# A 3136-point spectral block: the forward 49-point stage folded over n2 and -n2, in 50x50 products on quarters of the TensorE array

## The chip, the cores and the metric

One Trainium2 chip, one core. The metric is the device time of one execution in microseconds (us); the kernel before has a median of 1829.1 us over 3 runs (1829.03 to 1830.06). Everything is held and multiplied in 32-bit floats. The engines go by their names in the profile: PE is TensorE (matmul), PEld its weight loads, DVE VectorE, ACT ScalarE, POOL GpSimd, SP SyncE, which issues nearly all DMAs here.

## The reference, cut to what matters

The input x is 8 x 3136 x 256. A spectral filter runs along the sequence (a real FFT of 3136 points, a complex 256 x 256 product per frequency, a soft threshold, the inverse FFT); a second part takes the real part of a 2-D FFT of its result, normalises and applies a two-layer MLP.

```python
X = np.fft.rfft(x, axis=1)
Yr = X.real @ w_r - X.imag @ w_i + b_r
Yi = X.real @ w_i + X.imag @ w_r + b_i
Yr, Yi = shrink(Yr, 0.01), shrink(Yi, 0.01)
y = np.fft.irfft(Yr + 1j * Yi, n=3136, axis=1)
u = y + np.real(np.fft.fft(np.fft.fft(y, axis=1), axis=2))
un = (u - mean(u)) / sqrt(var(u) + 1e-6)
out = u + np.maximum(un @ w_ch1, 0) @ w_ch2
```

## The kernel before, in words

The 3136 points are taken as n = 49 n1 + n2, with 64 values of n1 and 49 of n2. For each of the 8 batches (`b`) these steps run; all of them are generators whose steps are put in order by due times (`T` is one batch in those units), and a scheduling layer that knows the waits then fixes one static order on each engine.

- **f1** (`p1`, and `p1_first` for the first batch): the 64-point transform over n1. `x` is loaded with n1 on the partitions (two halves of 64, for two sets of n2) into `xf`, multiplied by the table `fwd_f`, copied out of PSUM to `ev` (L522) and stored to DRAM as `ad`. From batch 2 on most f1 steps run as *quarter products* (`quads`, `run_quads`): four 64x64 products that use four quarters of the array at once, together with the four of an inverse step g1, under one start (L377 is the first product, L382 the others). Ahead of such a set `pair` writes one column of each of its two PSUM banks (L370) on DVE, so that the first product waits for both banks.
- **f2** (`p2_f2`): the 49-point transform over n2, for 32 values `u`. In each of 4 steps `q` it loads eight values of u: `af` (L584; 98 partitions, which are n2 by real and imaginary part, by 4 u x 256 channels) and the table `tff` (L580; 98 x 4 x 100). Each of `ui` = 0..3 fills one bank `g_f2` with four matmuls at L606: stationary `af` (98 x 128 channels), moving `tff` (98 x 100, real and imaginary outputs of 50 slots). A 32-bit matmul stands in the trace as two instructions, so 512 matmuls are 1024 rows of L606. Each bank is copied (`xx`, L629, or `im`, L644), split into a high part (`Xh`, L620) and a low part (`Xl`, L162 on POOL or L159 on DVE), and summed (`xs`, L636 or L645).
- **w** (`p2_w`): the 256 x 256 complex product, three terms each through `mm3` (L165 to L167).
- **mix, yt, g2, g1** (`p2_mix`, `p2_yt`, `p2_g2`, `p3_norm`): the channel FFT and the inverse transforms, with DRAM round trips `md`, `bd`. `bev` (L887) is the copy that is stored to `bd` (L889).
- **MLP** (`p3_tr`, `p3_mlp1`, `p3_mlp2`): `h` = W1 products (6 of 128x512 for one of eight `f`), ACT makes `hh` (L1055), DVE makes `hl` (L1056), and the 12 products into `o` use both.

The profile strips numbers from names: `g_f` is a bank of f1 or f2, `g_g` one of g1 or g2, `a` the `ad` of the first batch. All these banks come from one ring of four (`gtile`). The waits of one engine are in order: an instruction that waits holds all that stand behind it on that engine. SP is one such queue for loads and stores alike.

The lines that the steps of the prediction speak of, as they stand before:

```python
g = gtile("g_f2")
for s in range(2):
    for k in range(2):
        te.matmul(o, afs[s][:, ui * D + k * 128:ui * D + k * 128 + 128],
                  tfs[s][:, ui].rearrange("p (c j) -> p c j", c=2), start=True, stop=True)
```

Of the kernel before, what the change touches and what calls it, by code (L numbers as in the profile page):

```python
# [55 lines left out]
def rows_n2():  # L56

    return np.append(np.arange(48).reshape(2, 24).T.reshape(-1), 48)


def tables():
# [3 lines left out]
    fwd = np.zeros((2, N1, 2, 2, U))  # L65
    inv = np.zeros((2, 2, U, 2, 2, 32))
    n1h = rows_n1()
    for s in range(2):
        for u in range(U):
            ph = 2 * np.pi * ((n1 * u) % N1) / N1  # L70
            if u == 0:
                alt = np.where(n1 % 2, -1.0, 1.0)
                fwd[s, :, s, 0, 0] = 1.0
                fwd[s, :, s, 1, 0] = alt
                inv[s, 0, 0, :, s] = 1.0
                inv[s, 1, 0, :, s] = np.where(n1h % 2, -1.0, 1.0)
            else:
                fwd[s, :, s, 0, u] = np.cos(ph)
                fwd[s, :, s, 1, u] = -np.sin(ph)
# [3 lines left out]
    tf = np.zeros((2, N2, U, 2, S))  # L83
    ti = np.zeros((2, S, U, 2, N2))
    for u in range(U):
        t, sg = slot_freqs(u)
        m = len(t)
        ph = 2 * np.pi * (np.outer(n2, t) % N) / N
        co, si = np.cos(ph), np.sin(ph)
        if u == 0:  # L90
            for c in range(2):
                j = slice(25 * c, 25 * c + 25)
                tf[c, :, 0, 0, j] = co[:, j]
                tf[c, :, 0, 1, j] = -si[:, j]
                w = np.full(25, 2.0)
                w[0 if c == 0 else 24] = 1.0
                ti[0, j, 0, c] = (co[:, j] * w).T / N
                ti[1, j, 0, c] = (-si[:, j] * w).T / N
        else:
            tf[0, :, u, 0, :m] = co  # L100
            tf[1, :, u, 0, :m] = si
            tf[0, :, u, 1, :m] = -si * sg
            tf[1, :, u, 1, :m] = co * sg
            ti[0, :m, u, 0] = co.T / N
            ti[1, :m, u, 0] = -(si * sg).T / N
            ti[0, :m, u, 1] = si.T / N
            ti[1, :m, u, 1] = (co * sg).T / N
# [10 lines left out]
        tf=tf[:, rows_n2()].transpose(1, 0, 2, 3, 4).reshape(98, U, 100),  # L118
# [18 lines left out]
TURN = 0.2  # L137
EARLY, HALF = (2.03, 2.2, 2.36), 0.03
# [4 lines left out]
def spectral_block(ctx: ExitStack, tc: tile.TileContext, x, w_ri, b_ri, w1, w2,  # L143
# [123 lines left out]
    def load_tf():  # L267
        yield 0.31 * T
        for s in range(2):
            tff = sb.tile([98, 4, 100], F32, tag="tff", bufs=3, name="tff")  # L270
# [72 lines left out]
    def a_rows(t, n0, n):  # L343

        return t[n0 % 24:n0 % 24 + n, n0 // 24].rearrange("m c u d -> (c u) m d") if n0 < 48 else t[24:25, 0].rearrange("m c u d -> (c u) m d")

    def x_rows(b, m, n):

        if m == N2 - 1:
            return [xv[b + r][:, m:m + 1] for r in range(2)]  # L350
        return [xv[b][:, 24 * r + m:24 * r + m + n] for r in range(2)]

    def quads(gs, table, src):

        ops = []
        for k in range(2):
            rows = slice(64 * k, 64 * k + 64)
            for p in range(2):
                m = src[rows, p]
                o = gs[k][64 * p:64 * p + 64, :m.shape[1] * D].rearrange("q (i d) -> q i d", d=D)  # L360
                ops.insert(0, (o, table[rows, rows], m))
# [10 lines left out]
    def run_quads(ops, marks, key=None):  # L372
# [4 lines left out]
        mm = te.matmul(*ops[0], start=True, stop=True)  # L377
# [6 lines left out]
    chunks = [(m, 2) for m in range(0, NM - 1, 2)]  # L384

    def p1_first():
# [21 lines left out]
        todo = chunks + [(N2 - 1, 1)]  # L408
        xfs = []
        for (m, n), (tag, bufs, z, i) in zip(todo, slots):  # L410
            if i == 0:
                xf = sb.tile([128, z * 512], F32, tag=tag, bufs=bufs, name="xf")
            for r, src in enumerate(x_rows(0, m, n)):
                ld = (nc.scalar if r else nc.sync).dma_start(out=xf[r * 64:r * 64 + 64, i * 512:i * 512 + n * D], in_=src).ins
# [3 lines left out]
        for ci, (m, n) in enumerate(todo):  # L418
# [7 lines left out]
            mm = te.matmul(g[:, :w], fwd_0, xf[:, i * 512:i * 512 + w], start=True, stop=True)  # L426
# [6 lines left out]
            if i == z - 1:  # L433
# [3 lines left out]
                if n == 1:  # L437
                    for k, t in enumerate((a0, a8, a16, a24)):
                        o, i_ = t[24, 0].rearrange("c u d -> (c u) d"), ev[32 * k:32 * k + 16, :D]
# [4 lines left out]
                    for k in range(4):  # L444
                        later[3].append((ad1[24, 0, :, 8 * k:8 * k + 8], ev[32 * k + 16:32 * k + 32, :D]))
                    continue
                for k, t in enumerate((a0, a8, a16, a24)):
                    o, i_ = t[mb:mb + nn].rearrange("m r c u d -> (r c u) m d"), v[32 * k:32 * k + 32]
# [12 lines left out]
    def p1(b):  # L461
# [19 lines left out]

        def load(k):

            xfs[k] = sb.tile([128, 1024], F32, tag="x4", bufs=2, name="xf")
            for r in range(2):
                rows = slice(64 * r, 64 * r + 64)
                if k == 6:
                    behind(7, out=xfs[k][rows, :D], in_=xv[b + r][:, N2 - 1:])
                else:
                    ld = behind(5 if b == 1 else "mt" if b == 2 else 7, out=xfs[k][rows], in_=xv[b][:, 8 * k + 4 * r:8 * k + 4 * r + 4])  # L490
# [7 lines left out]
        for i, (t, k) in enumerate(order):  # L498
            yield t
            while b == 1 and (0, 2, 2) not in f2_mm:  # L500
# [4 lines left out]
            w = D if k == 6 else 512  # L505
            whole = k == 6 or b == 1 or keys[k] is None
            if not whole:
                gs, marks = pair("g_f1")
                waiting[keys[k]] = quads(gs, fwd_f, xf.rearrange("q (p i d) -> q p i d", p=2, d=D)), marks
# [3 lines left out]
            for r in range(2 - (k == 6)):  # L513
                if whole:
                    yield t + (F1_STEP if b == 1 else HALF) * T * r
                    g = gtile("g_f1")
                    with tc.issue_after(f2_mm[0, 2, 2]) if b == 1 and k == r == 0 else nullcontext():
                        te.matmul(g[:, :w], fwd_f, xf[:, r * 512:r * 512 + w], start=True, stop=True)
# [3 lines left out]
                (va.tensor_copy if r and whole and b > 1 else sc.copy)(ev[:, :w], g[:, :w])  # L522
                for p in range(2):
                    n2, n = 8 * k + (4 * p + 2 * r if whole else 4 * r + 2 * p), 2
                    ad = a_dram[b](0)[0]
                    if k == 6:
                        ad, n2, n = a_dram[b + p](0)[0], N2 - 1, 1
                    st_eng.dma_start(out=a_rows(ad, n2, n),
                                     in_=ev[p * 64:p * 64 + 64, :w].rearrange("p (n d) -> p n d", d=D))
# [25 lines left out]
    def p2_f2(b):  # L555


        for q in range(4):
# [6 lines left out]
            for s in range(2):  # L565
                roomy = b == 0 and q == 2
                if roomy:
                    if s == 0:
                        wide = sb.tile([98, 8 * D], F32, tag="mq", bufs=2, name="af")
                    af = wide[:, s * 4 * D:(s + 1) * 4 * D]  # L570
                else:
                    af = sb.tile([98, 4 * D], F32, tag="af", bufs=3, name="af")
# [3 lines left out]
                if not (b == q == 0):  # L576
                    tag, bufs = ("eo", 2) if roomy else ("bev", 3) if b == 0 and q == s == 1 else ("tff", 3)
                    tff = sb.tile([98, 4, 100], F32, tag=tag, bufs=bufs, name="tff")
# [4 lines left out]
                with tc.issue_after(af_ld["mt" if b else ("st", q - 1)]) if held else nullcontext():  # L583
                    ld = nc.sync.dma_start(out=af, in_=ad[:, :, :, u:u + 4].rearrange("m r c u d -> (m r c) (u d)")[0:98])  # L584
# [9 lines left out]
            for ui in range(4):  # L594
                yield base + STEP * ui * F2W / 4
                if b == 0 and q == 1:
                    yield from after(("w", 0))
                us = slice(ui * 2, ui * 2 + 2)
                g = gtile("g_f2")
                gv = g[:, :400].rearrange("p (k c t) -> p k c t", k=2, c=2)  # L600
                for s in range(2):
                    yield base + STEP * F2W * (ui / 4 + s / 8)
                    for k in range(2):
                        o = gv[:, k, :, s * S:s * S + S]
                        with tc.issue_after(last_mix[0]) if b == 1 and q == ui == 0 else behind_w(0, b == 0 and q == 1 and ui == 0):
                            f2_mm[b, q, ui] = te.matmul(o, afs[s][:, ui * D + k * 128:ui * D + k * 128 + 128], tfs[s][:, ui].rearrange("p (c j) -> p c j", c=2),  # L606
                                      start=True, stop=True).ins
                def put(f, outs, *ins, us=us):

                    both = len(outs[0]) == 1  # L610
                    for k in range(1 if both else 2):
                        v = [(t[0] if both else t[k])[..., us, :] for t in outs]
                        if not both:
                            i_ = [i[:, k] for i in ins]
                            d = "p u j -> p (u j)" if len(v[0].shape) == 3 else "p c u j -> p c (u j)"
                        else:
                            i_ = ins
                            d = "p k u j -> p k (u j)" if len(v[0].shape) == 4 else "p k c u j -> p k c (u j)"
                        v = [t.rearrange(d) for t in v]
                        res = f(v[0], *i_, *v[1:])  # L620
                    return res

                xs = sb.tile([128, 2, 2 * S], F32, tag="xs", bufs=2, name="xs")
                first = b == 1 and q == 0
                lag = b < 2 and q == 0
                if ui < (3 if b and not first else 2):
                    xx = sb.tile([128, 2, 2, 2 * S], F32, tag="xx", bufs=2, name="xx")
                    with tc.issue_after(ends["mix"][0]) if first else nullcontext():
# [540 lines left out]
```

## Time and profile before

| | us |
|---|---|
| median of 3 runs | 1829.1 |
| the profiled execution | 1830.16 |
| its span, first to last instruction | 1828.4 |
| PE busy | 1810.3 |
| DVE busy | 1179.5 |
| ACT busy | 834.6 |
| POOL busy | 370.3 |

The profiled execution is 1.1 us above the median, and 1.8 us of it lie outside the span. Shares of busy time are averages over the span; which engine sets the end in a stage is read from a table by stage (busy time of each engine in a window) and from the chain of waits, which goes back from the last instruction to what released each one. Ends of matmuls are modelled, so starts are the surer reading.

### The profile page before, as it was taken

What the parts mean: (1) busy time and instruction counts of PE and PEld (TensorE: products, weight loads), DVE (VectorE), ACT (ScalarE), POOL (GpSimd) and SP (SyncE); (2) the same over time, 40 slices, a digit from 0 to 9 for tenths busy, and PEclk for the clock granted to TensorE, in tenths of its full rate; (3) what the DMA queues carried; (4) which work ended last, traced back from release to release, by engine and by line L of the source; (5) the groups of instructions that cost most, each with busy time, mean ns of one, the idle gap of its engine ahead of it and who ended that gap; (6) DMA issues with size and microseconds to landing.
All of it is one profiled execution on the core that took longest, in us unless ns stands there. A gap on an engine that the chain in (4) does not pass through costs nothing.

```text
span 1828.4 us, 33511 instructions
## 1 busy us (share of the span) xinstructions
PE 1810.3 (99%) x12192; PEld 1597.3 (87%) x12192; DVE 1179.5 (65%) x2754; ACT 834.6 (46%) x1839; POOL 370.3 (20%) x805
## 2 busy tenths in 40 slices
PE   9999999999999999999999999999999999999999
PEld 6777889988999888988888988899899989888888
DVE  4776676766666766667666765766666667655442
ACT  3775554544444544444444444544444444422221
POOL 1522222221122222112222111222121222010000
PEclk9999999999999999999999999999999999999999
DMA  8879563544436453455434535454332543152100
GB/s 237 249 212 216 162 176 118 146 126 117 137 100 165 128 139 107 123 146 152 129 94 130 158 103 141 132 145 123 105 102 82 143 110 91 48 138 61 52 16 35
DMA packets 154877, 232.92 MB, mean 127 GB/s; under 512 B 18192, under 2 KB 108888, under 8 KB 154712
## 3 DMA queue, kind: packets, MB, share of 16 engines
q1 hardware_dynamic: 153672, 229.14, 44.8%
q8 instruction: 96, 1.57, 0.4%
q10 hardware_dynamic: 1040, 1.64, 0.3%
q14 instruction: 69, 0.57, 0.1%
HBM read 127.95 MB, written 102.76 MB: 126 GB/s over the span
## 4 chain that ended last, share of the span: by engine, by line
PE 95%; DVE 2%; DMA 1%; SPq 1%; ACT 1%; issue 0%; DVEq 0%; ACTq 0%
PE o L165 10%; PE o L166 10%; PE h L165 10%; PE h L167 10%; PE h L166 10%; PE o L167 10%; PE g_f L606 5%; PE g_w L165 4%; PE g_w L167 3%; PE g_w L166 3%; PE g_yt L854 3%; PE g_g L377 3%; PE g_ut L1030 2%; PE g_mix L771 2%; PE g_f L382 2%; PE g_g L165 1%
## 5 line engine op out<-in xcount | busy, mean ns | idle before, releaser
L1056 DVE SCALAR_TENSOR_TENSOR hl<-h,hh 128x512 fp32r<-128x512 f32 x392 | 269.9, 689 | 412.3 <-ACT hh L1055 410.3
L1055 ACT ACTIVATE hh<-h 128x512 fp32r<-128x512 f32 x392 | 234.3, 598 | 469.4 <-PE h L167 449.0
L166 PE MATMUL o<-w2h,hl 128*128 128x256 f32 x1568 | 432.0, 285 | 0.9 <-DVE hl L1056 0.9
L167 PE MATMUL o<-w2h,hh 128*128 128x256 f32 x1568 | 423.0, 280 | 0.0
L165 PE MATMUL o<-w2l,hh 128*128 128x256 f32 x1568 | 397.2, 287 | 0.0
L165 PEld LDWEIGHTS o<-w2l,hh 128*128 128x128 f32 x1568 | 283.6, 189 | 43.1 <-issue 23.5
L165 PE MATMUL h<-utl,w1h 128*128 128x512 f32 x784 | 314.4, 401 | 0.3 <-DVE utl L159 0.3
L167 PE MATMUL h<-uth,w1h 128*128 128x512 f32 x784 | 311.0, 397 | 0.0
L166 PE MATMUL h<-uth,w1l 128*128 128x512 f32 x784 | 310.5, 396 | 0.0
L166 PEld LDWEIGHTS o<-w2h,hl 128*128 128x128 f32 x1568 | 295.4, 188 | 6.9 <-DVE hl L1056 1.1
L167 PEld LDWEIGHTS o<-w2h,hh 128*128 128x128 f32 x1568 | 295.4, 188 | 2.7 <-issue 0.5
L167 PEld LDWEIGHTS h<-uth,w1h 128*128 128x128 f32 x784 | 147.4, 188 | 29.7 <-issue 1.1
L165 PEld LDWEIGHTS h<-utl,w1h 128*128 128x128 f32 x784 | 147.5, 188 | 21.4 <-DVE hl L1056 4.1
L166 PEld LDWEIGHTS h<-uth,w1l 128*128 128x128 f32 x784 | 147.7, 188 | 16.4 <-issue 0.2
L959 POOL TENSOR_SCALAR vv<-ag 128x2 f32<-128x2 f32 x98 | 18.9, 193 | 644.4 <-DVE ag L956 639.0
L606 PEld LDWEIGHTS g_f<-tff,af 98*128 98x128 f32 x1024 | 135.5, 192 | 9.3 <-issue 1.4
L606 PE MATMUL g_f<-tff,af 98*128 98x100 f32 x1024 | 140.5, 271 | 1.8 <-DMA af<-a 1.0
L162 POOL TENSOR_TENSOR Xl<-xx,Xh 128x400 fp32r<-128x400 f32 (+1 forms) x95 | 98.1, 1034 | 180.7 <-ACT Xh L620 177.8
L711 ACT ACTIVATE r<-g_w,two_t 128x400 f32<-128x400 f32 x128 | 76.1, 594 | 75.3 <-DVE g_w L707 71.0
L162 POOL TENSOR_TENSOR Xsl<-xs,Xsh 128x200 fp32r<-128x200 f32 x112 | 74.1, 664 | 166.7 <-ACT Xsh L620 163.0
L707 DVE SCALAR_TENSOR_TENSOR g_w<-g_w,bias,ks 128x400 f32<-128x400 f32 x128 | 81.4, 636 | 36.1 <-PE g_w L167 31.5
L159 DVE TENSOR_TENSOR yl<-g_yt,yh 100x512 fp32r<-100x512 f32 x112 | 76.6, 684 | 21.1 <-ACT yh L865 20.2
(160 smaller groups left out, 3281.0 us busy)
## 6 DMA issues: line engine op xcount, KB each, us to landing
bd<-bev SPq DMA_DIRECT2D x128, 196.0 KB
out_dram<-ut SPq DMA_DIRECT2D x98, 256.0 KB
bf<-bd SPq DMA_DIRECT2D x96, 256.0 KB
mt<-md SPq DMA_DIRECT2D x192, 128.0 KB
af<-ad SPq DMA_DIRECT2D x56, 392.0 KB
xf<-in_x SPq DMA_DIRECT2D x84, 256.0 KB
ad<-ev SPq DMA_DIRECT2D x168, 128.0 KB
md<-mq SPq DMA_DIRECT2D x112, 192.0 KB
```

The source lines that it names most:

```text
L159: return va.tensor_sub(out_, full, hi.bitcast(F32))
L162: gp.tensor_sub(out_, full, hi.bitcast(F32))
L165: te.matmul(o, lh, rl, start=start, stop=False)
L166: te.matmul(o, ll, rh, start=False, stop=False)
L167: return te.matmul(o, lh, rh, start=False, stop=stop)
L377: mm = te.matmul(*ops[0], start=True, stop=True)
L606: f2_mm[b, q, ui] = te.matmul(o, afs[s][:, ui * D + k * 128:ui * D + k * 128 + 128], tfs[s][:, ui].rearrange("p (c j) -> p c j", c=2), sta ...
L707: va.scalar_tensor_tensor(gw, gw, bias[:, c, o:o + 1], ks, op0=ALU.add, op1=ALU.add)
L711: ra = sc.activation(r, gw, AF.Relu, bias=lam_t)
L854: te.transpose(gt[:100, (v * 2 + o) * 128:(v * 2 + o + 1) * 128], y[:, o, place].rearrange("p c j -> p (c j)"), ident)
L1055: sc.activation(hh[:, :w], h[:, :w], AF.Relu)
L1056: dv = va.scalar_tensor_tensor(hl[:, :w], h[:, :w], 0.0, hh[:, :w].bitcast(F32), op0=ALU.max, op1=ALU.subtract)
```

## The change

The real input makes the terms n2 and -n2 = 49 - n2 combine: with e = x[n2] + x[-n2] and o = x[n2] - x[-n2], the 49 terms become 25 of e and 24 of o, each used with a cosine or a sine alone.

- **f2**: `af` and `tff` now hold 50 rows at partition 0 and 50 at partition 64 (the two come from the two kinds of output of f1), and a step `q` has two blocks `bi` in place of four `ui`. A block takes two banks at once (`pair`, with its two memsets), real outputs in one, imaginary in the other, and issues 32 quarter products (50 rows, 64 channels, 50 slots) through `run_quads`, one behind the other. Evictions work on 400 columns: copies `xi` and (first block) `xr`, then `Xh`, `Xl`, `xs`, `Xsh`, `Xsl`.
- **f1**: `xf` now pairs rows n2 and -n2 (the second read backwards). Where f1 runs as one 128-row product the table does the fold; where it runs as quarter products DVE does it (L517, L518: two instructions of 128x512, `FOLD` ahead of the step), and the load of `xf` is eight DMAs in place of two, since -n1 has an edge row. The single n2 = 0 (k = 6) is a product of 64 rows by 512 columns in place of 128 by 256.
- **DMAs**: `af` is two DMAs of 50 partitions in place of one of 98; the stores of `ev` are two per f1 step in place of four; `tff` has half the columns.

```diff
@@ tables()
-            tf[0, :, u, 0, :m] = co
-            tf[1, :, u, 0, :m] = si
-            tf[0, :, u, 1, :m] = -si * sg
-            tf[1, :, u, 1, :m] = co * sg
+            tf[0, 0:50:2, u, :z] = cm
+            tf[0, 1:50:2, u, :z] = sm
+            tf[1, 0:50:2, u, :z] = cm * sg
+            tf[1, 1:50:2, u, :z] = -sm * sg
...
+FOLD = 0.05
@@ run_quads
-    def run_quads(ops, marks, key=None):
+    def run_quads(ops, marks=(), key=None, last=None):
...
-        with tc.issue_after(mm.ins), tc.high_priority():
-            for o in ops[1:]:
-                te.matmul(*o, start=True, stop=True)
+        for o in ops[1:]:
+            with tc.issue_after(mm.ins), tc.high_priority():
+                mm = te.matmul(*o, start=True, stop=True)
+        return mm.ins
@@ p1: load
+            else:
+                for r in range(2):
+                    one, two = pairs(b, 4 * k + 1 + 2 * r, 2)[::1 - 2 * r]
+                    behind(key, out=xf[64 * r:64 * r + 64, 0:512], in_=one)
+                    lo, at = 64 * r, 512
+                    to, edge = (lo + 1, (lo, 63)) if r == 0 else (lo, (lo + 63, 0))
+                    behind(key, out=xf[to:to + 63, at:], in_=two[r:r + 63])
+                    for i in range(2):
+                        behind(key, out=xf[edge[0]:edge[0] + 1, at + i * D:at + i * D + D], in_=two[edge[1]:edge[1] + 1, i:i + 1])
@@ p1
+            if not whole(k):
+                yield t - FOLD * T
+                e, o = xfs[k][:, 0:512], xfs[k][:, 512:]
+                va.tensor_add(e, e, o)
+                va.scalar_tensor_tensor(o, o, -2.0, e, op0=ALU.mult, op1=ALU.add)
@@ p2_f2
-                    ld = nc.sync.dma_start(out=af, in_=ad[:, :, :, u:u + 4].rearrange("m r c u d -> (m r c) (u d)")[0:98])
+                    for h in range(2):
+                        ld = nc.sync.dma_start(out=af[64 * h:64 * h + 50], in_=ad[:, :, h, u:u + 4].rearrange("m t u d -> (m t) (u d)"))
...
-            for ui in range(4):
...
-                g = gtile("g_f2")
...
+            for bi in range(2):
...
+                gs, marks = pair("g_f2")
+                ops = []
+                for ui, s, k in ((ui, s, k) for ui in (2 * bi, 2 * bi + 1) for s in range(2) for k in range(2)):
+                    at, d0 = k * 4 * S + (2 * (ui % 2) + s) * S, ui * D + k * 128
+                    for h, p in ((h, p) for p in range(2) for h in range(2)):
+                        rows = slice(64 * h, 64 * h + 50)
+                        ops.append((gs[h][64 * p:64 * p + 64, at:at + S], afs[s][rows, d0 + 64 * p:d0 + 64 * p + 64], tfs[s][rows, ui]))
...
+                f2_mm[b, q, bi] = run_quads(ops, marks, last=behind_mm)
```

How this moves the static order is seen at two places, both in batch 4, step q = 2.

On PE before, the third of the four banks of this f2 step (`g_f_10629`), with what stands around it; `h`, `hh`, `hl`, `o` are the MLP's tiles:

```order
L167 MATMUL h<-uth,w1h 128x512
L606 MATMUL g_f_10629<-tff,af 128x2x50 [waits DVE_49]
L606 MATMUL g_f_10629<-tff,af 128x2x50 x3
L1030 MATMUL g_ut<-ident,ut 128x128 [waits DVE_49]
L165 MATMUL o<-w2l,hh 128x256 [waits Activation_49]
L165 MATMUL o<-w2l,hh 128x256
L1030 MATMUL g_ut<-ident,ut 128x128 x3
L166 MATMUL o<-w2h,hl 128x256 [waits DVE_49]
```

On PE now, the second block of the same step; the banks are `g_f_11549` and `g_f_11550`, and between the two parts shown stand 26 more rows like the four ahead of the cut:

```order
L165 MATMUL h<-uth,w1h 128x512
L374 MATMUL g_f_11549<-tff,af 64x50 [waits DVE_49]
L379 MATMUL g_f_11550<-tff,af 64x50 [waits Activation_49]
L379 MATMUL g_f_11549<-tff,af 64x50
L379 MATMUL g_f_11550<-tff,af 64x50
```

```order
L379 MATMUL g_f_11549<-tff,af 64x50
L379 MATMUL g_f_11550<-tff,af 64x50
L163 MATMUL o<-w2l,hh 128x256 [waits Activation_49]
L164 MATMUL o<-w2h,hl 128x256 [waits DVE_49]
```

The f2 work that stood in groups of one to sixteen among other products is now one unbroken block of 32 quarter products; here it stands alone between the last `h` product and the first `o` products, with one `o` product ahead of the one that waits for DVE's `hl`, where six other products stood before.

On DVE now, in the same step, a fold (L517) and the two memsets of the block shown above, with the rows between left as they are:

```order
L517 TENSOR_TENSOR xf<-xf 128x512 [waits DMAHW4_49,DMAHW5_49,DMAHW3_49,DMAHW6_49,DMAHW2_49,DMAHW7_49,DMAHW1_49,DMAHW0_49]
L1073 SCALAR_TENSOR_TENSOR hl<-h,hh 128x512 [waits Activation_49]
L157 TENSOR_TENSOR utl<-g_ut,uth 128x2x256 [waits Activation_49]
L366 MEMSET g_f_11415 128x1 [waits DVE_49]
L366 MEMSET g_f_11416 128x1 [waits DVE_49]
```

```order
L366 MEMSET g_f_11549 128x1 [waits DVE_49]
L157 TENSOR_TENSOR el<-eo,eh 128x400 [waits Activation_49]
L1073 SCALAR_TENSOR_TENSOR hl<-h,hh 128x512 [waits Activation_49]
L366 MEMSET g_f_11550 128x1 [waits Activation_49]
L657 TENSOR_TENSOR xs<-g_f_11415,xi 128x400 [waits Activation_49]
```

None of the L517 rows stood there before, and none of these four memsets. The fold waits for all eight pieces of its `xf`, and an `hl` stands right behind it; the last memset waits for an ACT copy out of the bank that it clears. On SP the later pieces of an `xf` stand behind a store of `bev`, as here (L329 is a load, L906 the store):

```order
L329 DMA xf_11706<-in_x 63x512
L906 DMA bd4_158<-bev_11268 98x512
L329 DMA xf_11706<-in_x 1x256 x2
```

## Rows read from the trace of the kernel before

**Rows 1.** The page: busy time by engine; the chain that ended last, by engine.

```profile
PE 1810.3 (99%) x12192; PEld 1597.3 (87%) x12192; DVE 1179.5 (65%) x2754; ACT 834.6 (46%) x1839; POOL 370.3 (20%) x805
PE 95%; DVE 2%; DMA 1%; SPq 1%; ACT 1%; issue 0%; DVEq 0%; ACTq 0%
```

**Rows 2.** Windows: stretch, length, busy us (instructions) PE PEld DVE ACT POOL, clock, DMA.

```profile
0.00:152.00 152.00, 138.41 (x706) 109.99 (x707) 101.83 (x228) 90.35 (x225) 48.60 (x59) 0.98 0.83 230
152.00:1540.00 1388.00, 1388.00 (x9600) 1237.73 (x9602) 929.86 (x2184) 663.47 (x1456) 297.95 (x642) 1.00 0.46 130
```

**Rows 3.** The same windows, of line L606 alone: busy us (instructions) PE, PEld.

```profile
0.00:152.00 152.00, 20.18 (x160) 19.90 (x160) 0.98 0.83 230
152.00:1540.00 1388.00, 120.34 (x864) 115.56 (x864) 1.00 0.46 130
```

**Rows 4.** The chain around 16 instructions of f2: start us, us, what.

```profile
936.12 0.24 PE o L165 x2
...
936.69 1.76 PE g_f L606 x16
938.46 0.15 PE o L166
938.61 0.12 PE o L167
```

**Rows 5.** The chain around a set of quarter products (g1, f1).

```profile
924.31 0.23 PE h L167
924.54 0.57 PE g_g L377
...
925.13 0.41 PE g_g L377
...
925.56 0.86 PE g_f L382 x8
926.42 0.45 PE o L165 x2
```

**Rows 6.** The timeline of PE's weight loads there: start us, us, engine, line.

```profile
924.47 0.13 PEld L377 LDWEIGHTS g_g<-bf,inv_f 64*64 64x64 f32 x1 [0.36 <-issue]
924.48 0.14 PEld L382 LDWEIGHTS g_g<-bf,inv_f 64*64 64x64 f32 x3
924.53 0.13 PEld L377 LDWEIGHTS g_g<-bf,inv_f 64*64 64x64 f32 x1
924.53 0.15 PEld L382 LDWEIGHTS g_g<-bf,inv_f 64*64 64x64 f32 x3
```

**Rows 7.** Groups by line and shape: count, busy us, mean ns, idle ahead.

```profile
L518 PE MATMUL g_f<-xf,fwd_f 128*128 128x512 f32 x36 | 18.6, 602 | 0.0
L518 PE MATMUL g_f<-xf,fwd_f 128*128 128x256 f32 x6 | 1.8, 388 | 0.0
L243 DVE SCALAR_TENSOR_TENSOR wsf<-wi,wrf 128x512 f32<-128x512 f32 x1 | 0.7, 693 | 1.4 <-DMA wi<-in_w_ri 1.4
L370 DVE MEMSET g_g<- 128x1 f32 x96 | 5.3, 59 | 5.2 <-ACT ks L690 2.5
L162 POOL TENSOR_TENSOR Xl<-xx,Xh 128x400 fp32r<-128x400 f32 x87 | 92.2, 1061 | 170.6 <-ACT Xh L620 167.7 <-issue 2.7
L162 POOL TENSOR_TENSOR Xsl<-xs,Xsh 128x200 fp32r<-128x200 f32 x112 | 74.1, 664 | 166.7 <-ACT Xsh L620 163.0 <-DMA af<-a 3.7
```

**Rows 8.** The timeline of ACT and DVE behind the `h` product that ends in [rows 5].

```profile
924.64 0.60 ACT L1055 ACTIVATE hh<-h 128x512 fp32r<-128x512 f32 x1 [2.23 <-PE h L167]
...
925.27 0.69 DVE L1056 SCALAR_TENSOR_TENSOR hl<-h,hh 128x512 fp32r<-128x512 f32 x1 [2.13 <-ACT hh L1055]
```

**Rows 9.** The chain in the first stage: SP's issues, and transfers from issue to landing.

```profile
17.56 2.78 DMA a<-ev
...
20.47 0.33 SPq L584
...
20.85 0.38 SPq L584
...
41.70 4.91 DMA a<-ev
...
136.48 4.36 DMA mt<-md
```

**Rows 10.** SP's own waits: who waited for whom, us in total, times, longest.

```profile
SPq L889 <- DVE bev L887: 317.6, 64, 12.7
```

More of the change, by code (lines that the diff above doesn't have):

```diff
@@ L425, in p1_first @@
                 keep_busy(8)
-            mm = te.matmul(g[:, :w], fwd_0, xf[:, i * 512:i * 512 + w], start=True, stop=True)
+            rows = slice(0, 128 if m else 64)
+            mm = te.matmul(g[:, :w], fwd_0[rows], xf[rows, i * 512:i * 512 + w], start=True, stop=True)
             if ci == len(todo) - 1:
@@ L513, in p1 @@
             for r in range(2 - (k == 6)):
[L514 removed]
+                if whole(k):
                     yield t + (F1_STEP if b == 1 else HALF) * T * r
                     g = gtile("g_f1")
[L517 to L518 removed]
+                    with tc.issue_after(f2_mm[0, 2, 1]) if b == 1 and k == r == 0 else nullcontext():
+                        rows = slice(0, 64 if k == 6 else 128)
+                        te.matmul(g, fwd_f[rows], xf[rows, r * 512:r * 512 + 512], start=True, stop=True)
                 else:
@@ L521, in p1 @@
                 ev = sb.tile([128, 512], F32, tag="ev", bufs=EVB, name="ev")
[L522 to L529, printed above, removed]
+                (va.tensor_copy if r and whole(k) and b > 1 else sc.copy)(ev, g)
+                v = ev.rearrange("p (n d) -> p n d", d=D)
+                if k == 6:
+                    for c in range(2):
+                        st_eng.dma_start(out=a_rows(a_dram[b + c](0)[0], 0, 1), in_=v[:, c:c + 1])
+                else:
+                    st_eng.dma_start(out=a_rows(a_dram[b](0)[0], 4 * k + 1 + 2 * r, 2), in_=v)
         done.add(("a", b))
@@ new lines, in p2_f2 @@
+                xi = sb.tile([128, 2, 4 * S], F32, tag="im" if bi else "xx", bufs=1 if bi else 2, name="xi")
+                with tc.issue_after(ends["mix"][0]) if first else nullcontext():
+                    sc.copy(xi, gi)
+                re, im = (gr, lo_v), (xi, lo_g)
+                if bi == 0:
+                    xr = sb.tile([128, 2, 4 * S], F32, tag="xx", bufs=2, name="xr")
+                    re = (xr, lo_g)
+                    sc.copy(xr, gr)
+                    if q == 0:
+                        sc.copy(xi[:, :, 25:50], gr[:, :, 25:50])
+                        sc.copy(xr[:, :, 25:50], gi[:, :, 25:50])
+                elif lag:
+                    im = (gi, lo_v)
@@ L648, in p2_f2 @@
+                with tc.issue_after(ends["mix"][1]) if first else nullcontext():
+                    va.tensor_add(xs, xr if q == 0 and bi == 0 else gr, xi)
+                todo = [(put, c) + v for c, v in ((1, im), (0, re))]
+                if not lag:
+                    for put, c, v, lo in todo:
+                        ac = put(sc.copy, [Xh], v, c)
+                        dv = put(lo, [Xl, Xh], v, c)
                 ac = put(sc.copy, [Xsh], xs)
                 sl = put(lo_v if lag else lo_g, [Xsl, Xsh], xs)
-                if ui == 3:
-                    for put, lo, v in later_h:
+                later_h += todo
```

175 lines of the change are left out of this document (74 added, 101 removed).

## The prediction

> **What bounds the kernel now.** I read the page first, then the windows, then the chain at two places of the middle. PE is busy for 1810.3 us of a span of 1828.4 and holds 95% of the chain [rows 1]. That is a mean, so the windows come next [rows 2]: from 152 to 1540 us PE is busy for the whole 1388.00 us, at the full clock (1.00), while DVE has 929.86 us (67%) and the DMA engines a share of 0.46. In that stage a microsecond less for PE is a microsecond less for the kernel, as long as nothing else comes late. In the first 152 us PE is busy for 138.41 and the DMA engines for a share of 0.83; f2's products there wait for transfers that the chain shows one behind the other, issue and landing [rows 9]. What PE saves on f2 there is not counted. Of the 1024 rows of f2's products, 864 lie in the middle and 160 in the first stage [rows 3]; none is left after 1540.
>
> The tick for this kernel is 0.2%, or 3.7 us: less than that a measurement can hardly tell from no change.
>
> **f2's products before.** In the chain 16 of them take 1.76 us [rows 4], 0.11 each; the `o` behind them takes 0.15 and the next one 0.12, so leaving f2 costs 0.03. The 864 are 54 sets of 16, and 54 x 1.79 = 96.7 us.
>
> **f2's products after.** One set of 16 becomes one block of 32 quarter products, 64 instructions, 16 groups of four that use four quarters together. Two prices are needed.
>
> A group of four. What limits it is the loading of weights or the streaming of 50 columns. Loads: four loads of 64 columns start at 924.47 to 924.48 and the next four at 924.53 [rows 6], so a group's loads take 0.05 to 0.06 us; that is half of the 0.11 of a 128-column load. Streaming: two groups of 512 columns take 0.86 us [rows 5], so 50 columns take 0.43 x 50/512 = 0.042. The bounds are 0.042 below (loads quite hidden) and 0.11 above (four small loads as dear as one of today). I take 0.055, the row of the very same loads. A block's groups take 16 x 0.055 = 0.88 us.
>
> Going into and out of quarters. The first group of such a set takes 0.57 us where an equal one inside takes 0.41, and the `o` pair behind it takes 0.45 where the pair ahead of f2 takes 0.24 [rows 4, 5]: 0.16 + 0.21 = 0.37 us.
>
> A block is 1.25 us, 54 blocks are 67.5, and f2 gains **29.2 us**. The bounds of the group's price move this by -11.2 us of time (0.013 x 16 x 54) and, if 0.11 held, +47.5, which is a loss.
>
> *A rule against the change.* That 0.055 needs the loads of a group to go on beside the products of the group ahead of it, which sit in the same quarters. The trace shows this twice: the second four loads start at 924.53, before the first group has run [rows 5, 6], and today's f2 takes 0.11 where a load of 0.11 and a stream of 100 columns (0.084) one after the other would be 0.19 [rows 4]. The Trainium skill ("TensorE: Matmul & The Clock Gate", Part 3 on packing small matmuls) says that a weight load overlaps with products in flight only when its row group is another one. By that rule the time would be that of rival B; by the rows it is the sum here. The trace disagrees with the rule, as far as these two places go.
>
> **Less cover for `hl`.** f2 stood in pieces among the MLP's products and is now one block. After an `h` has ended (924.31 + 0.23 = 924.54), ACT needs 0.60 and DVE 0.69 until 925.96 [rows 5, 8]: 1.42 us. In the new order there are 10 places, the one shown among them, where only the block and one `o` stand in that gap: about 1.25 + 0.12 = 1.37, and the weights of the waiting `o` are loaded beside the one ahead of it. Four more are a little short. Before, no place was as short. At 0.05 to 0.3 us each I take **+2 us** (bounds 0 and +6).
>
> **n2 = 0.** Six instructions of 128x256 (0.388) become six of 64x512, for which the row of 128x512 stands (0.602) [rows 7]: 6 x 0.214 = **+1.3 us** on PE.
>
> **The first stage.** Every `af` load is one more issue on SP, 0.33 to 0.38 us each in the chain [rows 9], and there are eight of them in that batch (some 3 us at most, part of it under the landing of the one ahead); evictions run on 400 columns in place of 200, so the first of each pair is ready later (`Xl` 1.06 against `Xsl` 0.66 on POOL [rows 7]); against that, `tff` is half as wide and fewer stores of `ev` go out, where DMA is the bound. I take **+3 us**, bounds -3 and +10 (one landing of 4 to 5 us twice later).
>
> **What costs nothing, and its cover.** DVE gets 33 folds of two instructions, each priced like the same operation on 128x512, 0.69 us [rows 7]: 45.5 us; and 128 memsets at 0.059, 7.6 us. Most lie in the middle, where DVE is at 67% [rows 2]: it goes to about 70%, as the wider evictions save a few instructions. The 96 memsets of L370 of today waited only 5.2 us in all [rows 7]. Without that cover each fold would cost 1.4 us of PE, 45 us. SP issues 1426 DMAs in place of 1248: 178 x 0.35 = 62 us of its time, against 317.6 us in which it stands waiting for `bev` alone [rows 10]. Cover gone there means late `xf` pieces, which is the next point.
>
> **The wait that is added: the fold.** On DVE the fold waits for all eight pieces of its `xf` and holds what stands behind it, in the order shown an `hl`. In 26 of the 33 cases the last pieces stand on SP behind a store of `bev`, whose copy on DVE is only 4 to 14 rows ahead of the fold. At 0.43 us a row (929.86/2184 [rows 2]) that is 1.7 to 6.0 us, and from the copy to the landing go three issues (1.0) and a transfer of 2.8 to 4.9 [rows 9]: 3.8 to 5.9. So some folds stop DVE for some us. PE sees it only where DVE's slack is used up: at [rows 5] `hl` is needed after 926.42 + 0.45 = 926.87 and could be done at 925.96, a slack of 0.9, and a third of DVE's time is idle to catch up. Bounds 0 (all covered) and rival A. I take **+4 us**, two or three stops of 1.5 to 2 us, nearer to nothing because the memsets, whose waits in order are of the same kind, cost 5.2 us in all.
>
> **Sum** on the profiled execution: 1830.2 - 29.2 + 2 + 1.3 + 3 + 4 = 1811.3. It is 1.1 above the median of the runs, so the forecast is **1810 us**.
>
> **The rivals.**
>
> *A, the fold holds DVE (slower).* From the middle of those numbers: copy to fold 9 rows, 3.8 us; issues and landing 1.0 + 4.4; DVE waits 1.6, `hl` comes 1.6 + 0.69 = 2.3 later, PE loses 2.3 - 0.9 = 1.4. At 26 folds that is 36 us in place of the 4: about **1842**. It decides from (29.2 - 6.3)/26 = 0.9 us of PE lost per fold. For it: the order on SP and DVE. Against it: the DMA engines are at 0.46 there, so landings will be nearer to 2.8 than to 4.9, and at most places more products stand ahead of the `o` than at [rows 5].
>
> *B, loads do not run beside products of their own quarters.* A group costs 0.055 + 0.042 = 0.097, 54 x 16 x 0.042 = 36 us more: about **1846**. The gain of the sum is gone at 0.077 per group (18.9/864 above 0.055). The upper bound 0.11 of a group's price lies beyond it, with B's chance. Against it: the two places above.
>
> *C, the four quarters do not run together at this size.* A group costs four streams or loads in a row, 0.22: 54 x (3.52 + 0.37) - 96.7 = 113 us, about **1950** with the rest. Against it: sets of 512 columns do run together, 0.86 for eight [rows 5].
>
> *D, the gain is given back at the banks.* A block takes two banks of a ring of four at once and starts only when both are empty, with a memset behind each copy. If each of the 54 waits two thirds of a copy like ACT's 0.60 [rows 8], 0.4 us, 21.6 us are lost: about **1832**, no difference. Against it: the 5.2 us of the memsets of today [rows 7].
>
> **How the numbers follow.** The forecast's case gets 0.74, A 0.10, B 0.06, C 0.02, D 0.08. Its own range is 1793 (group at 0.042, first stage at -3) to 1825 (first stage at +10, `hl` at +6, folds at +8). The range reaches on to D, to 1834, and leaves out A, B and C (0.18) and a little below. Faster by over 0.2% is the first case, 0.74; within 0.2% is D, 0.08; slower are A, B and C, 0.18.
>
> **What the profile after would show.** Right: the chain or the timeline has blocks of 64 instructions of L374 and L379 at 0.9 us plus 0.2 at the start and 0.2 in the `o` behind; PE's busy time in the middle falls by 25 to 30 us and stays within a few us of that stage's length; DVE about 70% busy. A: idle time of DVE ahead of L517, released by a DMA of `xf`, of 40 us or more, and PE's `o` (L164) waiting for `hl`. B: a block of 1.55 us and PE with no idle time. C: a block of 3.5 us. D: idle time ahead of L366 and PE waiting at L374. The first stage is wrong if it ends more than 10 us later than before. The forecast falls if a block takes over 1.7 us, or if PE's idle time in the middle is over 20 us.

## The result and the profile after

The changed kernel has a median of 1853.4 us over 4 runs (1851.65 to 1857.26) against 1829.6 for the kernel before: a ratio of 1.0133, 95% interval 1.0116 to 1.0151. It is **24 us slower**; 1810 was forecast, in a range of 1793 to 1834. The profiled execution has a span of 1849.9 us, 21.5 longer than before.

Busy time by engine and the chain by engine, from the page of the changed kernel, are the counterpart of [rows 1]:

```profile
PE 1803.1 (97%) x15264; PEld 1555.3 (84%) x15264; DVE 1205.3 (65%) x2875; ACT 821.2 (44%) x1755; POOL 351.4 (19%) x746
PE 77%; DMA 10%; DVE 7%; SPq 2%; issue 1%; ACT 1%; DVEq 0%; ACTq 0%
```

PE is busy for 7 us less in a span that is 21 us longer, and DMA and DVE have come into the chain. The same two windows as [rows 2] (stretch, length, busy us of PE, PEld, DVE, ACT, POOL, clock, DMA share):

```profile
0.00:152.00 152.00, 134.63 (x1162) 102.39 (x1162) 95.23 (x209) 87.40 (x203) 46.34 (x52) 0.94 0.76 221
152.00:1540.00 1388.00, 1362.93 (x11951) 1183.88 (x11952) 948.72 (x2293) 641.48 (x1367) 273.33 (x583) 1.00 0.44 128
```

In the middle PE had no idle time; now it has 25 us. The groups by line and shape (count, busy us, mean ns, idle time of the engine ahead and what ended it) show which instruction on DVE waits:

```profile
L517 DVE TENSOR_TENSOR xf<-xf 128x512 f32<-128x512 f32 x33 | 22.7, 688 | 58.8 <-DMA xf<-in_x 27.5 <-DMA mt<-md 26.3 <-DMA af<-ad 2.3
L518 DVE SCALAR_TENSOR_TENSOR xf<-xf 128x512 f32<-128x512 f32 x33 | 22.6, 683 | 0.2
L164 PE MATMUL o<-w2h,hl 128*128 128x256 f32 x1568 | 432.9, 285 | 10.7 <-DVE hl L1073 9.1
```

The 33 folds take 45.3 us of DVE's time (22.7 + 22.6), as forecast, but DVE stands idle for 58.8 us ahead of them, and PE's `o` waits 9.1 us for `hl`, where before it waited for 0.9 us. 19 of the folds waited; each of these starts 2.1 to 3.1 us after the last piece of its `xf` was issued on SP, so they waited for their own pieces; the `mt` in the line is a load that SP issued just behind the last piece.

Where the loss is, in order of time. The sets of quarter products that g1 and f1 run are the same in both kernels; the starts of the first and the last set (first and last start of L377 before, then of L374 now) and of the third set, near 200 us:

```profile
L377 PE MATMUL g_g<-bf,inv_f x96: 589/615/641, 156.4 to 1742.0; 64*64 64x512 f32 x96
191.07 0.57 PE g_g L377
```

```profile
L374 PE MATMUL g_g<-bf,inv_f x96: 589/600/640, 163.1 to 1763.6; 64*64 64x512 f32 x96
208.73 0.57 PE g_g L374
```

The first set is 6.7 us late, the one near 200 us 17.7, the last 21.6. So 11 us go within one interval of about 40 us; after it another 4 are lost, though f2's gain, over 20 us, lies there. The chain through that interval:

```profile
143.86 5.37 DMA bf<-bd
149.25 2.22 DMA xf<-in_x
151.64 0.69 DVE xf L517
152.33 0.66 DVE utl L157
153.04 0.50 PE h L163
...
155.37 0.43 PE h L163
...
166.93 7.89 DMA bf<-bd
174.84 0.61 SPq L329
175.50 3.23 DMA xf<-in_x
179.04 0.69 DVE xf L517
...
180.81 0.61 DVE yl L157
181.47 0.53 PE g_g L163
```

Twice a load of `xf` stands on SP behind a load of `bf`, the fold waits for it, and `utl` and `yl`, which have nothing to do with it, wait behind the fold with PE waiting for them. On DVE, the second wait is 8.34 us long:

```profile
179.04 0.69 DVE L517 TENSOR_TENSOR xf<-xf 128x512 f32<-128x512 f32 x1 [8.34 <-DMA xf<-in_x]
```

PE stood for 1.9 us before the `h` of 153.04 and for 5.0 before the `g_g` of 181.47. The clock falls for a while with each of the two stops: `h` products took 0.43 us instead of 0.23 after the first (1.2 in place of 2.4 GHz), and the granted clock is 0.91 from 140 to 160 and 0.66 from 180 to 190, means over both levels, where e8_late3_b2 below, which has neither stop, shows 1.00 for both:

```profile
140.00:160.00 20.00, 17.16 (x81) 14.13 (x80) 16.72 (x38) 7.83 (x17) 4.43 (x7) 0.91 0.87 220
180.00:190.00 10.00, 8.53 (x97) 7.18 (x98) 5.00 (x10) 4.35 (x9) 3.07 (x3) 0.66 0.37 107
```

From batch 3 on five waits of 4.1 to 6.4 us come back at the same place, one per batch; they are the 26.3 us that the line puts down to `mt`. Here pieces of `xf` stand on SP behind a store of `bev`, as the prediction showed:

```profile
590.90 0.67 DVE L904 COPY bev<-g_g 98x512 f32<-98x512 f32 x1
597.20 0.92 SPq L906 DMA_DIRECT2D bd<-bev  x1
598.17 2.06 SPq L329 DMA_DIRECT2D xf<-in_x  x5
602.64 0.69 DVE L517 TENSOR_TENSOR xf<-xf 128x512 f32<-128x512 f32 x1 [6.38 <-DMA mt<-md]
```

The copy ended at 591.57, but SP, with other DMAs ahead, issued its store only at 597.20. PE makes up for most of such a wait: behind this one it stood for 0.69 and 0.91 us.

Later a fold does harm without a wait too. The chain at a place that comes back nine times:

```profile
629.80 0.67 DVE mq L800 x2
630.48 0.60 DVE xf L517
631.08 0.61 DVE hl L1073
631.73 0.39 PE o L164
```

The load has landed, but the fold stands ahead of the `hl` that PE waits for: 0.92 us of idle time of PE, 8.3 in the nine places. This is the 15th of the 33 folds, and the loads go through two buffers in turn, so it is the 15th set of f1's quarter products that reads it, 59 us later:

```profile
689.55 1.04 PE L379 MATMUL g_f<-xf,fwd_f 64*64 64x512 f32 x8
```

PE's 25 us of idle time in the middle are thus about 6 behind the two waits at the start (a part of the first stop lies before 152), 8.3 behind folds that had not waited, and some 11 in other short stops, most of them just behind a fold that had.

### The profile page after: what moved, and what is told of

Its sections match the earlier page's. It is cut to its first block, busy times and chain, and to the rows that moved or that the text cites. A ratio compares the mean times of both kernels' runs of the same rounds, so it can differ in the third digit from the quotient of the medians.

```text
span 1849.9 us, 39709 instructions
## 1 busy us (share of the span) xinstructions
PE 1803.1 (97%) x15264; PEld 1555.3 (84%) x15264; DVE 1205.3 (65%) x2875; ACT 821.2 (44%) x1755; POOL 351.4 (19%) x746
## 4 chain that ended last, share of the span: by engine, by line
PE 77%; DMA 10%; DVE 7%; SPq 2%; issue 1%; ACT 1%; DVEq 0%; ACTq 0%
PE o L164 9%; PE o L163 9%; PE h L163 8%; PE h L164 8%; PE h L165 8%; PE o L165 8%; PE g_w L163 3%; PE g_f L379 3%; PE g_w L165 3%; PE g_w L164 3%; PE g_yt L871 2%; DMA xf<-in_x 2%; PE g_g L374 2%; DMA bf<-bd 2%; PE g_ut L1047 2%
## 5 line engine op out<-in xcount | busy, mean ns | idle before, releaser
L163 PE MATMUL o<-w2l,hh 128*128 128x256 f32 x1568 | 403.1, 287 | 0.1
L160 POOL TENSOR_TENSOR Xl<-xi,Xh 128x400 fp32r<-128x400 f32 (+1 forms) x66 | 68.1, 1035 | 197.8 <-ACT Xh L639 154.7
L1097 DVE SCALAR_TENSOR_TENSOR ut<-o,rs,ut 128x256 f32<-128x256 f32 x196 | 82.7, 474 | 12.7 <-PE o L165 12.6
L871 PE MATMUL g_yt<-ident,Y 128*100 128x128 f32 x512 | 85.3, 274 | 3.2 <-DVE Y L729 1.5
L802 POOL TENSOR_TENSOR mq<-mq 100x508 f32<-100x508 f32 x28 | 41.2, 1471 | 247.1 <-DVE g_f L366 125.9
L729 DVE SCALAR_TENSOR_TENSOR Y<-g_w,r 128x400 f32<-128x400 f32 x128 | 72.9, 570 | 22.3 <-ACT r L728 20.9
```

Of the source, the lines that this page charges most:

```text
L160: gp.tensor_sub(out_, full, hi.bitcast(F32))
L163: te.matmul(o, lh, rl, start=start, stop=False)
L729: ya = va.scalar_tensor_tensor(y[:, o, :, c, :], gw, LAM, r, op0=ALU.add, op1=ALU.min)
L871: te.transpose(gt[:100, (v * 2 + o) * 128:(v * 2 + o + 1) * 128], y[:, o, place].rearrange("p c j -> p (c j)"), ident)
L1097: va.scalar_tensor_tensor(ut[:, j], o[:, j * D:j * D + D], rs[:, j], ut[:, j], op0=ALU.mult, op1=ALU.add)
```

## The experiments

**Theory 1**: DVE, in order, is held by the fold; 1a by its wait for the load, 1b by its 1.4 us of work. **Theory 2**: the unbroken f2 block and its two banks. **Theory 3**: the eight pieces of `xf`.

**e1_nofold**, without the fold:

```diff
-                va.tensor_add(e, e, o)
-                va.scalar_tensor_tensor(o, o, -2.0, e, op0=ALU.mult, op1=ALU.add)
```

> The two fold instructions on DVE are left out in all 33 places (the quarter products of f1 then read the loaded rows unfolded); the loads stay as they are. Theory 1, DVE held by the fold: idle of PE in the middle (19 us) and the two long gaps near 150 and 176 us go, and the time falls by 25 to 40 us, to 1813 to 1828. Theory 2, the unbroken f2 block and its two banks are what costs: the time stays within 8 us of 1853. Theory 3, late pieces of xf: PE now waits for the pieces itself at L374, and the time falls by 5 to 15 us only.

1822.5 us, ratio to the kernel before 0.9965 (0.9953 to 0.9976): 31 us less than the changed kernel, as theory 1 said. Theory 2 falls, and so does theory 3 as it was put, as the eight pieces are still loaded.

**e2_pool**, the fold on POOL:

```diff
-                va.tensor_add(e, e, o)
-                va.scalar_tensor_tensor(o, o, -2.0, e, op0=ALU.mult, op1=ALU.add)
+                gp.tensor_tensor(o, e, o, op=ALU.subtract)
+                gp.tensor_tensor(e, e, e, op=ALU.add)
+                gp.tensor_tensor(e, e, o, op=ALU.subtract)
```

> The fold is moved from DVE to POOL, as three operations on 128x512 (about 4 us in all) in place of two. Theory 1: DVE is no longer held, and the time falls by 20 to 35 us, to 1818 to 1833, unless the later xf makes the quarter products wait. Theory 2: within 8 us of 1853. Theory 3: a fall of 5 us at most, since the pieces are as late as before and the fold is longer.

1852.9 us (ratio 1.0124, 1.0108 to 1.014): no gain, and no verdict for theory 2 or 3, because something new took the place of the wait. The timeline of DVE and then of POOL in this kernel:

```profile
626.26 2.55 DVE L801 TENSOR_TENSOR mq<-mq 100x256 f32<-100x256 f32 x2
628.73 0.68 DVE L1074 SCALAR_TENSOR_TENSOR hl<-h,hh 128x512 fp32r<-128x512 f32 x1
626.06 1.28 POOL L517 TENSOR_TENSOR xf<-xf 128x512 f32<-128x512 f32 x1 [4.84 <-DMA bd<-bev]
```

The two `mq` operations on DVE take 2.55 us beside POOL's fold, where the changed kernel shows them at 0.67 (the chain above), and `hl` is late again: PE waits 20.5 us for `hl` in this run. The Trainium skill ("SBUF — State Buffer", the section on its two separate sides) says that a DVE operation with two SBUF inputs and a GpSimd operation that reads SBUF lock each other out of a shared port pair for the whole instruction; the 2.55 us agree.

At the start the wait moved along with the fold: POOL stands for 10.29 us at the second fold, `Xl` and `Xsl` stand behind it, and PE waits for `Xsl`:

```profile
180.46 1.29 POOL L517 TENSOR_TENSOR xf<-xf 128x512 f32<-128x512 f32 x1 [10.29 <-DMA tff<-c_tf]
189.44 0.70 PE L163 MATMUL g_w<-Xsl,wrh 128*128 128x400 f32 x1 [4.32 <-POOL Xsl L160]
```

**e3_twodma**, the load of a folded `xf` as two DMAs:

```diff
-                for r in range(2):
-                    one, two = pairs(b, 4 * k + 1 + 2 * r, 2)[::1 - 2 * r]
...
+                for r, src in enumerate(pairs(b, 4 * k + 1, 4)):
+                    ld = behind(key, out=xf[64 * r:64 * r + 64], in_=src)
```

> Each xf that is folded is loaded by two DMAs in place of eight (the rows then don't stand in the order that the fold wants, so the values differ); the folds stay on DVE. Theory 3, the wait for the last pieces: DVE's idle time ahead of L517 (54 us) falls to under 20 and the time by 15 us or more. Theory 1 in the form that DVE's own 1.4 us per fold costs, not the wait: the time falls by under 8 us. Theory 2: no change.

1943.0 us (ratio 1.0619, 1.0603 to 1.0635): worse by 90, which no theory had. The fold (now L508) waits longer, not shorter:

```profile
L508 DVE TENSOR_TENSOR xf<-xf 128x512 f32<-128x512 f32 x33 | 22.9, 692 | 119.1 <-DMA xf<-in_x 102.2 <-DMA mt<-md 13.4 <-issue 3.4
152.00:1540.00 1388.00, 1314.10 (x11271) 1136.57 (x11272) 888.91 (x2149) 603.12 (x1288) 253.33 (x545) 0.96 0.42 120
```

Twice the wait at the fold, 74 us of idle time of PE in the middle, and a granted clock of 0.96 there. So fewer pieces are no cure, and that eight pieces cost little where the fold doesn't wait for them is shown by e8_late3_b2 below, which loads them too (theory 3 falls). Here most folds that wait start 4.4 to 7.8 us after the last issue, against 2.1 to 3.1; that issue is 256 KB, while the last of the eight pieces is 1 KB. Whether the size is the reason was not tried.

**e4_b2whole**, no fold in batch 2:

```diff
-            return k == 6 or b == 1 or keys[k] is None
+            return k == 6 or b <= 2 or keys[k] is None
```

> The three f1 steps of batch 2 that ran as folded quarter products run as whole 128-row products with the fold in the table: 3 x 0.86 us more of PE, no fold in the first 300 us. If the two folds near 150 and 180 us hold DVE behind SP's loads of bf, the 7 us of idle and about 4 us of lowered clock there go, and the time falls by 6 to 10 us, to 1843 to 1847. If those gaps come from the transfers of bf themselves, they stay, and the time rises by 0 to 3 us.

1856.2 us (ratio 1.0143, 1.0125 to 1.016): no gain in the total, where 6 to 10 us were expected, but the start did what was expected. The set that began at 191.07 before and at 208.73 in the changed kernel begins here at

```profile
193.56 0.57 PE g_g L374
```

and the loss comes back behind the folds that follow, one of which waits 5.1 us at 270. Mending one stop was not enough while the next folds still waited.

**e5_nomem**, an f2 block without its two memsets:

```diff
-                gs, marks = pair("g_f2")
+                gs, marks = [gtile("g_f2") for _ in range(2)], ()
```

> The two memsets ahead of each f2 block are left out; the products then wait for their banks themselves, the second bank from within the block. Rival D, the pair of banks costs 0.2 to 0.4 us per block: a fall of 8 to 20 us. The other theories: within 5 us of 1853.

1859.5 us (ratio 1.0165, 1.0142 to 1.0188): no fall, so the memsets' waits are not the price. The two banks are still taken at once here; but in the changed kernel all of PE's waits for DVE ahead of an f2 block (L374 into `g_f`) come to 2.5 us, where rival D needed 21.6, so D is out. The rise of 6 is taken up by e12_nomem_b2.

**e7_late3** and **e7_late6**, the fold later on DVE (`FOLD` 0.03 or 0.06):

```diff
-                va.tensor_add(e, e, o)
+                with tc.issue_after(ends["last_hl"]) if "last_hl" in ends else nullcontext():
+                    va.tensor_add(e, e, o)
...
+                ends["last_hl"] = dv.ins
```

> From batch 3 on each fold is put behind the last hl that stands in the program 0.03 of a batch ahead of its step, so that on DVE it comes some 20 to 25 us later than now and still ahead of its use (now it stands where its load lands, 16 to 34 us ahead of PE's use in most places). The four folds ahead of the first hl keep their place. Theory 1a, DVE loses time by waiting for the load at the fold: the gaps ahead of the fold in the middle go (they are 54 us in all, about 14 of them in the first two), and the time falls by 10 to 20 us, to 1833 to 1843. Theory 1b, DVE's own 1.4 us per fold is what costs: the time stays within 5 us of 1853.

> The same with 0.06 of a batch: folds some 15 us later than now. Theory 1a: like the run with 0.03, within 4 us. Theory 1b: within 5 us of 1853. If the place among other DVE work (an hl right behind a fold) is what decides, the two runs differ by more than 5 us.

1832.5 us (1.0017, 1.0007 to 1.0026) and 1830.9 (1.0006, 0.9997 to 1.0016): 21 and 23 us less than the changed kernel by the place of 30 folds. The 16 to 34 us of the expectation are the distance to the next f1 set, and not to the one that reads the fold; matched in order, as above, the folds from batch 3 on stand 27 to 75 us ahead of their use in the changed kernel (25 of 30 at 50 to 67), and in e7_late3 28 of 30 at 6 to 13. The edit moves the fold away from its load's landing and puts it behind an `hl`, so how much of the gain is the wait and how much the place, the runs don't separate. What is left of the waits at the fold are the two at the start: in e7_late3

```profile
L518 DVE TENSOR_TENSOR xf<-xf 128x512 f32<-128x512 f32 x33 | 25.0, 757 | 11.0 <-DMA xf<-in_x 11.0
```

**e8_late3_b2**, e7_late3 and e4_b2whole together:

> The later folds (0.03) and batch 2 without folds (its three f1 steps as whole products, 2.6 us more of PE). Theory 1a: the start loses nothing (5 us behind the kernel before at 200 us, where the changed kernel was 17 behind) and keeps it, as the folds behind it no longer wait: 1820 to 1830. Theory 1b: 1838 to 1850.

1822.1 us (ratio 0.9958, 0.9943 to 0.9973), 31 less than the changed kernel and 7.6 less than the kernel before: the version that beats both. No fold waits, and the middle is PE's again but for 4 us (groups by line, windows, waits):

```profile
L518 DVE TENSOR_TENSOR xf<-xf 128x512 f32<-128x512 f32 x30 | 23.4, 779 | 0.0
152.00:1540.00 1388.00, 1384.02 (x12268) 1208.65 (x12267) 971.36 (x2333) 652.40 (x1397) 285.81 (x600) 1.00 0.44 129
PE o L164 <- DVE hl L1074: 3.6, 10, 0.7
```

DVE does more work in that window than in the changed kernel (971.4 against 948.7, as more of the program fits in), and PE's `o` waits for it for 3.6 us in all. **e9_late6_b2** is the same with 0.06:

> The kernel with later folds and batch 2 without folds, with 0.06 of a batch in place of 0.03. If the exact place of the later folds matters little, the same within 3 us of that run's 1822; as 0.06 was 1.7 us faster than 0.03 with batch 2 folded, 1820 to 1822 is likeliest.

1823.3 us (0.997, 0.9958 to 0.9981): which of the two places is taken does not matter once the fold doesn't wait.

**e11_nofold_b2**, e8_late3_b2 without the other 30 folds:

> The kernel with later folds (0.03) and batch 2 without folds, the other 30 folds left out (the quarter products of f1 read unfolded rows). It tells what a fold costs once it doesn't wait. Theory 1a, only the wait costs: within 4 us of 1822. Theory 1b, DVE's 1.4 us per fold cost too: 1802 to 1816.

1824.2 us (0.9971, 0.9962 to 0.998): leaving them out gains nothing. Theory 1b falls: 60 DVE instructions, 44 us, are free where they don't wait and don't stand ahead of a waited-for `hl`.

**e12_nomem_b2**, e8_late3_b2 with the edit of e5_nomem:

> The kernel with later folds (0.03) and batch 2 without folds, without the two memsets ahead of each f2 block. If the rise of the first run without memsets (1859.5 against 1853.4) is the price of a block that waits in its midst for its second bank, it shows here too: 1825 to 1831. If it came from folds that fell on other places, the time stays within 3 us of 1822.

1823.0 us (0.9964, 0.9951 to 0.9977): the memsets cost nothing either way. In e5_nomem the waits at the folds had grown from 58.8 to 66.7 us, which fits its rise.

**e10_half**, the f2 products of e8_late3_b2 on half arrays:

```diff
-                    for h, p in ((h, p) for p in range(2) for h in range(2)):
+                    for h in range(2):
                         rows = slice(64 * h, 64 * h + 50)
-                        ops.append((gs[h][64 * p:64 * p + 64, at:at + S], afs[s][rows, d0 + 64 * p:d0 + 64 * p + 64], tfs[s][rows, ui]))
+                        ops.append((gs[h][:, at:at + S], afs[s][rows, d0:d0 + 128], tfs[s][rows, ui]))
```

> On the kernel with later folds (0.03) and batch 2 without folds: each f2 block as 16 products of 50 rows by 128 channels in place of 32 of 50 by 64, on the upper and the lower half of the array. Theory of the sum: a group of four quarters costs half of a 128-column load, 0.055 us; with 128-column loads the 32 instructions of a block cost 0.11 each if the two halves load one after the other (3.5 us a block, 54 x 2.4 = 130 us more, 1950), 0.11 a pair if they load together (1.76 us, 37 us more, 1859). Rival: the loads are hidden either way and the columns streamed decide (2 x 50 columns a pair, as for quarters): no change, 1818 to 1826.

1875.8 us (ratio 1.0257, 1.0238 to 1.0276), 54 more than e8_late3_b2, though the columns streamed are the same: the weight loads set the price, and the two halves' loads go together. From the first product of a block to the `o` behind it a block takes 971.57 to 973.49 = 1.92 us against 1.08; 54 blocks by 0.84 are 45 us of the 54; the other 9 were not traced. Its timeline of PE:

```profile
971.57 0.31 PE L374 MATMUL g_f<-tff,af 50*128 50x50 f32 x1
...
971.73 1.83 PE L379 MATMUL g_f<-tff,af 50*128 50x50 f32 x29
973.49 0.38 PE L164 MATMUL o<-w2h,hl 128*128 128x256 f32 x1
```

In order of DVE's idle time at the fold: 0.0 us (e8_late3_b2) 1822.1, 9.5 (e7_late6) 1830.9, 11.0 (e7_late3) 1832.5, 50.6 (e4_b2whole) 1856.2, 58.8 (the change) 1853.4, 66.7 (e5_nomem) 1859.5, 119.1 (e3_twodma) 1943.0. The times follow but for e4_b2whole, whose `o` waits 14.5 us for `hl` against 9.1 in the changed kernel.

## Why the prediction was wrong, point by point

**f2's blocks: right.** The timeline of PE at one block of the changed kernel:

```profile
963.37 0.49 PE L871 MATMUL g_yt<-ident,Y 128*100 128x128 f32 x3
963.79 0.26 PE L374 MATMUL g_f<-tff,af 50*64 50x50 f32 x1
...
963.89 1.05 PE L379 MATMUL g_f<-tff,af 50*64 50x50 f32 x59
964.87 0.38 PE L164 MATMUL o<-w2h,hl 128*128 128x256 f32 x1
965.09 0.28 PE L165 MATMUL o<-w2h,hh 128*128 128x256 f32 x1
965.21 0.28 PE L163 MATMUL o<-w2l,hh 128*128 128x256 f32 x1
```

From 963.79 to 964.87 are 1.08 us. The `o` behind takes 0.22 where the next takes 0.12, and the three transposes ahead 0.42 (963.37 to 963.79) where 0.33 is usual: 1.27 us in all, against 1.25 in the sum. In single rows the groups of four start every 58 ns from the second on; 0.055 was taken. The gain by this is 54 x (1.79 - 1.27) = 28 us, 29.2 in the sum. Rivals B (0.097 a group) and C are out. The Trainium skill ("TensorE: Matmul & The Clock Gate", Part 3 on packing small matmuls) says that a weight load overlaps with products in flight only when its row group is another one. The trace disagrees: 58 ns is the price of a group's loads alone, with nothing added for the stream.

**The fold: the step that failed.** The sum had **+4 us** for the wait that is added, "two or three stops of 1.5 to 2 us", priced by the memsets. It cost 31 us (1853.4 to 1822.1, and the 1822.1 holds 2.6 us of dearer products besides). The prediction's own signs say the same: 58.8 us of DVE's idle time ahead of L517, where 40 was the sign of A, and 25 us of PE's in the middle, where 20 was the limit. Rival A named the mechanism and gave 1842 and a chance of 0.10.

The place of the wait was half right: stores of `bev` stand ahead of the pieces in the five waits of 26.3 us, but at the start it is loads of `bf`, and those two waits were the dearest, 11 us with the lowered clock. The working had 3.8 to 5.9 us from the end of the `bev` copy to the landing. Where the fold didn't wait it was 4.0 to 5.2 us in 13 of 14 places; in the five waits it was 8.7 to 11.1 us (591.57 to 602.64 above), as SP did not issue the store at once. (The 0.43 us a row of that working is DVE's busy time alone; with its idle time a row of that stage is 0.64, 1388/2184, so the gap between copy and fold is taken too short there.) Nor was PE's loss behind waits alone: 8.3 us came behind folds whose load had landed.

The argument against rival A failed too: a low mean share of the DMA engines (0.46) says nothing of one load that stands in line on SP, where its issue is late rather than its transfer slow. What the order shown could have told is that the fold stood where its load was expected to land, 27 to 75 us ahead of its use from batch 3 on: any delay of the load was a delay of DVE, with no need for it.

**Cover of `hl`: right in size without the fold.** +2 was taken; in e8_late3_b2 `o` waits 3.6 us for `hl`, in the changed kernel 9.1, 8.3 of them with a fold ahead of it.

**What costs nothing: right for the work, wrong for the wait.** The 45 us of folds and the memsets are hidden (e11_nofold_b2, e12_nomem_b2). The text said that without cover late `xf` pieces come next; it priced that too low.

**n2 = 0: right.** 641 ns against 388 for six instructions, 1.5 us:

```profile
L537 PE MATMUL g_f<-xf,fwd_f 64*128 64x512 f32 x6 | 3.4, 641 | 0.0
```

**First stage: within its bounds, its size not settled.** +3 was taken, -3 to +10 bounded; the first set of quarter products is 6.7 us late, of which the first fold's 1.9 us of idle time is a part. The granted clock of the first 152 us is 0.94 against 0.98, some 6 us (an estimate, 152 x 0.04). In e8_late3_b2, with no fold there, the set is 2.2 us early (154.2), in e1_nofold, with none either, 5.4 late (161.8); so one trace each does not fix this term.

**What stays open.** Without the fold's 4 us, and with the 2.6 us of e8_late3_b2, the sum gives 1809.9 on the profiled execution; that of e8_late3_b2 took 1819.9, 10 more (its median, 1822.1, is above that). Its page and its windows:

```profile
PE 1789.2 (98%) x15252; PEld 1548.4 (85%) x15252; DVE 1207.8 (66%) x2866; ACT 817.2 (45%) x1752; POOL 353.9 (19%) x746
0.00:152.00 152.00, 131.51 (x1168) 99.32 (x1169) 97.82 (x216) 87.80 (x205) 46.08 (x52) 0.98 0.78 224
```

In a span of 1818.1 us PE is idle for 28.9, 10.8 more than before; 6.9 of these lie in the first 152 us and 4.0 in the middle, and the sum had 5 for both. That is 5.8 of the 10. PE's busy time fell by 21.1 where the sum has 25.3 (29.2 - 1.3 - 2.6), the other 4.2; f2's gain of 28 in place of 29.2 is a part, and some 3 us of busy time have no place yet.

## What to carry to other kernels

An operation that waits for a load on an in-order engine costs that engine all that stands behind it, so it belongs shortly ahead of its use and not where its data is expected to land; the time between the two is free cover. Here moving 30 folds of two instructions from (for most) 50 to 67 us ahead of their use to 6 to 13 was worth 21 us. It also belongs behind, not ahead of, an instruction that another engine is about to need: nine folds that had not waited cost 8.3 us. A mean share of DMA busy time does not bound the lateness of one load: look at what stands ahead of it on the queue that issues it, and at what that waits for. Here small products were priced by the length of one weight load, and quarters of the array loaded together (58 ns a group).

## What the runs showed of the hardware that was not expected

The price of a group of small products was the length of a single load, not the sum of its loads: 16 groups of four 64-column loads took 1.08 us and 16 pairs of 128-column loads 1.92, though both load the same weights and stream 50 columns each. POOL's work on SBUF tensors stops some of DVE's: two `mq` operations that take 0.67 us took 2.55. And the two stops of PE, of 1.9 and 5.0 us, were paid twice: a stretch at half the clock came with each (`h` products of 0.43 us in place of 0.23 behind the first).
